# Chunked attention and an MLP on one core: pairs 3 to 5 in 64-token chunks, early transposes on another queue

## The chip, the core and the metric

The kernel runs on one core of a Trainium2 chip. The metric is the device time of one execution in microseconds. The kernel before took 215.75 us in the median of three runs (215.47 to 216.52); the profiled execution spans 214.9 us. TensorE (PE in the profile) multiplies, VectorE (DVE), ScalarE (ACT) and GpSimd (POOL) do elementwise work, SyncE (SP) issues DMAs.

## The reference

The inputs are q, k and v of 4 batches x 8 heads x 768 tokens x 64 numbers, a decay lam for each head, and the weights of an MLP with 512 inputs and 2048 hidden units. First comes a linear attention with decay, in blocks of 64 tokens with a state of 64 x 64 for each batch and head:

```
Dmask = where(rel >= 0, lam ** rel, 0)
for each block of 64 tokens:
    intra = ((qb @ kb.T) * Dmask) @ vb
    inter = (qb * lam ** (pos + 1)) @ kv_state
    out   = intra + inter
    kv_state = lam ** 64 * kv_state + (kb * lam ** (63 - pos)).T @ vb
```

The heads are then joined to rows x of 512 numbers, and each row gets a residual MLP: out = x + relu(norm(x) * g @ w1) @ w2, where norm takes off the mean and divides by the standard deviation. The reference fixes the result, not the chunk: a chunk of 128 tokens gives the same numbers as two of 64.

## The kernel before, in words

**Pairs.** The work is cut into 12 pairs (the code's u, from 0 to 11; NU is 12). A pair is 256 tokens of one batch with all heads, as two tiles of 128 rows (ab = 0 and 1). Pairs 0 to 3 are the first 256 tokens of the four batches, 4 to 7 the next, 8 to 11 the last. Pair u needs the state that pair u - 4 left.

**Two forms of the attention.** LB = 6 (L56) picks the form: pairs below it work in chunks of 128 tokens, the others in chunks of 64. In the long form, `kv` (L281) makes the state's update, `scores` (L247, two calls of 16 matmuls with 128 columns) the products of k and q, `mask` (L257) multiplies with the causal mask, `av` (L393, 64 matmuls) multiplies with v, and `inter` (L406) adds what the state gives. In the short form these are `kv64` (L346), `scores64` (L327, 32 matmuls with 64 columns), `mask64` (L333), `av64` (L380, 32 matmuls), `inter`, and `states64` (L362, L365, L287, L370), which makes a state between the chunks too. All use 64 x 64 tiles of TensorE. LB also picks how q, k and v are loaded (`fill`): below it one DMA for each tensor, with two neighbouring tokens in a partition, so rows of 512 bytes (L71); from it on two DMAs for each tensor with rows of 256 bytes (L75). `in_k`, `in_q` and `in_v` (L199, L210, L216) turn the loaded tensors to bf16, with the powers of the decay multiplied in, on GpSimd for most pairs.

**Transposes.** Attention needs k and q transposed (kqT), the MLP needs the normalised rows transposed (xT from xc). From pair 2 (xT) and pair 3 (kqT) on these are DMA transposes that SyncE issues (`to_xT`, L451; `transpose_dma`, L231), in its one queue with the loads and the stores of the output (L550), in the order of the code. [...]

**The MLP.** The two tiles of a pair make a group. `m1` has 8 units of 16 matmuls with 256 columns (L484), each followed by a relu on ScalarE (hT, L487). `m2` has 8 units of 4 matmuls with 512 columns (L522), four for each tile; after the last of a tile VectorE makes o (L543), for which `rstd_of` has to have made the standard deviation on ScalarE (std, L461) and its reciprocal on VectorE (L463). pm of both, kv64's pk and the scores of some early pairs take turns in the four PSUM buffers "mm" of `mm_tile`; a matmul that begins a new tile waits until the tile four before it in that round was read.

**The order.** There is no scheduler: the instructions of each engine run in the order in which the code records them. At the end of the kernel a list `plan` holds the units of the MLP, 16 for each group from number 22 on (group 2: 22 to 37, group 3: 38 to 53, group 4: 54 to 69), and `add(n, ...)` hangs the steps of attention, loads and transposes behind unit n. Pairs 3 to 5 have their pieces at several such places (`s1`, `s2`, `s3`, `s4`; loads by `load_one`, preparation by `p0`). Pairs from 6 on have one step, `X`, which does the end of pair u - 1 and the beginning of pair u; for pair 6 it is split into `X1` and `X2`. `wind_up` does the end of the last pair. In it a second PSUM tile, rest, takes the state's part of the odd half. `make_keep64` makes the mask of the short form on GpSimd, at unit 34.

Of the kernel before, what the change touches and what calls it, by code (L numbers as in the profile page):

```python
# [10 lines left out]
ALU = mybir.AluOpType  # L11
# [5 lines left out]
def kernel(  # L17
# [11 lines left out]
    nc = tc.nc  # L29
    B, H, S, D = q.shape  # L30
# [3 lines left out]
    NU = B * S // W  # L34
# [18 lines left out]

    half = [slice(0, 64), slice(64, 128)]
    XB = 3
    LB = 6  # L56

    def mm_tile(shape, dtype, name):
        return ps.tile(shape, dtype, tag="mm", bufs=4, name=name)
# [135 lines left out]
    def in_k(u, eng, hs=ALL):  # L195
        src = qkv_in[u]["k"][:, hs].rearrange("p (a e) j d -> p a e j d", e=2)
        dst = part(0, st[u]["kq"], hs)
        for j in range(2):
            (eng.copy if eng is nc.scalar else eng.tensor_copy)(dst[:, :, :, j], src[:, :, :, j])  # L199

    def in_q(u, eng, hs=ALL):
        src = qkv_in[u]["q"][:, hs].rearrange("p (a e) j d -> p a e j d", e=2)
        dst = part(1, st[u]["kq"], hs)
        if u < LB:
            lq = lam_q[:, hs, :].rearrange("p (a e) j -> p a e j", e=2)
        else:
            lq = lam_p[:, 0:1, hs].rearrange("p j (a e) -> p a e j", e=2).to_broadcast([128, (hs.stop - hs.start) // 2, 2, 2])
        n = (hs.stop - hs.start) // 2
        for j in range(2):
            eng.tensor_tensor(dst[:, :, :, j], src[:, :, :, j],  # L210
                              lq[:, :, :, j:j + 1].to_broadcast([128, n, 2, D]), op=ALU.mult)

    def in_v(u, eng, hs=ALL):
        n = hs.stop - hs.start
        lv = lam_v[:, hs, :, None] if u < LB else lam_p[:, 1, hs, None, None]
        eng.tensor_tensor(st[u]["vb"][:, hs], qkv_in[u]["v"][:, hs], lv.to_broadcast([128, n, 2, D]), op=ALU.mult)  # L216
# [10 lines left out]
    def transpose_dma(u):  # L227
        s = st[u]
        s["kqT"] = wk.tile([128, 2, NP, 2, 128], BF16, tag="kqT", bufs=3, name="kqT")
        for a in range(2):  # L230
            nc.sync.dma_start_transpose(s["kqT"][:, a].rearrange("p b j t -> p (b j) t"),  # L231
                                        s["kq"][:, a].rearrange("p b j e d -> p (b j e d)"))

    def scores(u, hf, early=False):
# [96 lines left out]
    def mask64(u, e):  # L331
        s = st[u]
        nc.vector.tensor_tensor(s["mA"][:, e], s["sc"][e],  # L333
                                keep64[:, None, None, :].to_broadcast([128, NP, 2, D]), op=ALU.mult)

    def kv64(u):
        s = st[u]
        last = (u // B + 1) * W >= S
        s["pk"] = [mm_tile([128, 2, NP, D], F32, f"pk{ab}") for ab in range(2)]
        n_j = (2, 1 if last else 2)  # L340
        for j in range(2):
            for p in range(NP):
                for e in range(2):
                    for ab in range(2):
                        if j < n_j[ab]:
                            nc.tensor.matmul(s["pk"][ab][half[e], j, p, :], lhsT=s["kq"][half[ab], 0, p, j, e],  # L346
                                             rhs=s["vb"][half[ab], 2 * p + e, j], start=(p == 0 and j == 0),
                                             stop=(p == NP - 1 and j == n_j[ab] - 1), skip_group_check=True)
# [93 lines left out]
    def to_xT(u, ab):  # L442
        s = st[u]
        t = 2 * u + ab
        g = group_of[t]
        i = t - groups[g][0]
        if i == 0:
            xT_of[g] = gp.tile([128, KA, GT * 128], BF16, tag="xT", bufs=3, name="xT")
        dst = xT_of[g][:, :, i * 128:(i + 1) * 128]
        if u >= 2:  # L450
            nc.sync.dma_start_transpose(dst, s["xc"][:, ab])  # L451
        else:
            xt = mm_tile([128, KA, 128], BF16, "xt")
# [243 lines left out]
    def p0(u, k_eng=None):  # L697
# [2 lines left out]
        in_q(u, nc.gpsimd)  # L700
        in_v(u, nc.gpsimd)

    def s0(u):
        kv(u, "po")
        new_state(u, 0, nc.gpsimd)
        new_state(u, 1, nc.gpsimd)
# [13 lines left out]
    def wind_up(u):  # L720


        s = st[u]
        if u < LB:
            av(u, range(NP))
        else:
            av64(u)
        inter(u, 0, fence=False)
        qT = s["kqT"][:, 1]
        has = [s["S"][ab][1] is not None for ab in range(2)]  # L730
        rest = [ps.tile([128, H, D], F32, tag="sc", bufs=2, name=f"rest{ab}") if has[ab] else None for ab in range(2)]
        for p in range(NP):
            for jq in range(2):
                for e in range(2):
                    ab = 1 - e
                    if s["S"][ab][jq] is not None:
                        nc.tensor.matmul(rest[ab][half[jq], 2 * p + e, :], lhsT=qT[half[e], p, jq, half[ab]],
                                         rhs=s["S"][ab][jq][half[e], p, :],
                                         start=(p == 0), stop=(p == NP - 1), skip_group_check=True)
        s["x"] = xp.tile([128, 2, DM], F32, tag="x", name="x")  # L740
        s["mv"] = xp.tile([128, 2, 2], F32, tag="mv", name="mv")
        s["xc"] = wk.tile([128, 2, DM], BF16, tag="xc", name="xc")
        for ab in range(2):
            x, xh = s["x"][:, ab], s["x"][:, ab].rearrange("p (a e d) -> p a e d", e=2, d=D)
            nc.scalar.copy(x, s["po"][ab].rearrange("p h d -> p (h d)"))
            if has[ab]:

                odd = xh[:, :, 1 - ab]
                nc.vector.tensor_tensor(odd, odd, rest[ab].rearrange("p (a e) d -> p a e d", e=2)[:, :, 1 - ab], op=ALU.add)
            stats = wk.tile([128, 6], F32, tag="stats", name="stats")  # L750
            nc.vector.bn_stats(stats, x)
            nc.vector.bn_aggr(s["mv"][:, ab], stats)
            nc.vector.scalar_tensor_tensor(s["xc"][:, ab], in0=x, scalar=s["mv"][:, ab, 0:1], in1=g_row,
                                           op0=ALU.subtract, op1=ALU.mult)
# [88 lines left out]
    def add(at, *steps):  # L843
        after.setdefault(at, []).extend(steps)
# [5 lines left out]
    add(6, (s2, 2))  # L850
    add(8, (s0, 2))
    add(10, (s3, 2))
    add(12, (s4, 2), (p4, 2), (p0, 3, nc.vector), (transpose_dma, 3))
    for n, name in zip((14, 15, 16), "kqv"):
        add(n, (load_one, 5, name))
    add(15, (rstd_of, 2))
    add(17, (p0, 4))
    add(25, (s1, 3))
    add(25, (transpose_dma, 4))
    add(27, (s2, 3))  # L860
    add(28, (p0, 5))
    add(29, (s3, 3))
    add(30, (s4, 3), (p4, 3))
    for n, name in zip((30, 31, 32), "kqv"):
        add(n, (load_one, 6, name))
    add(34, (rstd_of, 3), (make_keep64,))
    add(37, (transpose_dma, 5))
    add(38, (s1, 4))
    add(39, (p0, 6))
    add(40, (s2, 4))  # L870
    add(42, (s3, 4))
    add(44, (s4, 4), (p4, 4))
    add(46, (transpose_dma, 6))
    add(50, (s1, 5), (rstd_of, 4))
    add(53, (s2, 5))
    for j in range(6, NU):
        at = 55 + 16 * (j - 6)
        if j > 6:
            for n, name in zip((23, 21, 19), "kqv"):
                add(at - n, (load_one, j, name))  # L880
            add(at - 13, (p0, j))
            add(at - 8, (transpose_dma, j))
        if j < LB:
            add(at, (s1_s3, j))
            add(at + 4, (s2_s4, j), (p4, j - 1))
        else:
            if j == 6:
                add(at + 1, (X1, j))
                add(at + 5, (X2, j), (p4, j - 1))
            else:  # L890
                add(at + 2, (X, j), (p4, j - 1))
        add(at + 9, (rstd_of, j - 1))
    add(151, (wind_up, NU - 1), (p4, NU - 1))
    add(159, (rstd_of, NU - 1))
# [32 lines left out]
```

## Time and profile before

| what | value |
|---|---|
| median of three runs | 215.75 us (215.47 to 216.52) |
| TensorE busy in the profile | 201.9 us, 94% of the span |
| VectorE, ScalarE, GpSimd busy | 102.9, 87.1, 79.4 us |
| DMA queue of SyncE (q1) | 32.38 MB, 71.4% of 16 engines' span |
| chain that ended last | TensorE 75%, DMA 13%, GpSimd 4% |
| matmuls of the MLP (L484, L522) | 86.3 and 81.1 us |
| length of groups 2, 3, 4 (55.02 to 106.11 us) | 17.00, 17.91, 16.18 us |
| length of groups 5, 6, 7 | 15.36, 15.22, 15.26 us |

The length of a group is the time from its first L484 matmul to that of the next group. Groups 5 and later hold one pair of the short form each; groups 2 to 4 hold the pieces of pairs 3 to 5 and the beginning of pair 6. In the answers shown below, an arrow in brackets names what ended an engine's idle time, and the chain is followed back from the last instruction: each piece is either work or a wait for what the piece names.

### The profile page before, as it was taken

What the parts mean: (1) busy time and instruction counts of PE and PEld (TensorE: products, weight loads), DVE (VectorE), ACT (ScalarE), POOL (GpSimd) and SP (SyncE); (2) the same over time, 40 slices, a digit from 0 to 9 for tenths busy, and PEclk for the clock granted to TensorE, in tenths of its full rate; (3) what the DMA queues carried; (4) which work ended last, traced back from release to release, by engine and by line L of the source; (5) the groups of instructions that cost most, each with busy time, mean ns of one, the idle gap of its engine ahead of it and who ended that gap; (6) DMA issues with size and microseconds to landing.
All of it is one profiled execution on the core that took longest, in us unless ns stands there. A gap on an engine that the chain in (4) does not pass through costs nothing.

```text
span 214.9 us, 6642 instructions
## 1 busy us (share of the span) xinstructions
PE 201.9 (94%) x2884; PEld 138.2 (64%) x2899; DVE 102.9 (48%) x225; ACT 87.1 (41%) x165; POOL 79.4 (37%) x111
## 2 busy tenths in 40 slices
PE   2989999999799999999999999999999999999992
PEld 0568788454674675585585685784784874866861
DVE  3678461565168436747347256174183292522011
ACT  4765679120442244055063162261370460731600
POOL 4747139039464173229019138056065020000000
PEclk9999999999999999999999999999999999999998
DMA  4999999999999898799799999998998511320303
GB/s 130 289 272 207 219 263 160 236 284 234 215 303 208 169 229 153 110 215 209 126 220 199 137 230 200 177 203 198 206 246 131 128 27 27 99 52 0 98 3 95
DMA packets 94142, 37.13 MB, mean 173 GB/s; under 512 B 68385, under 2 KB 91169, under 8 KB 94114
## 3 DMA queue, kind: packets, MB, share of 16 engines
q1 hardware_dynamic: 89584, 32.38, 71.4%
q0 software_dynamic: 4224, 4.19, 12.4%
q8 instruction: 22, 0.36, 0.7%
q10 hardware_dynamic: 306, 0.14, 0.3%
q14 instruction: 6, 0.05, 0.1%
HBM read 27.27 MB, written 6.29 MB: 156 GB/s over the span
## 4 chain that ended last, share of the span: by engine, by line
PE 75%; DMA 13%; POOL 4%; SPq 3%; DVE 2%; issue 1%; POOLq 0%
PE pm L484 35%; PE pm L522 30%; DMA vin<-in_v_dram 6%; DMA qin<-in_q_dram 4%; SPq L71 3%; DMA kqT<-kq 2%; POOL kq L210 2%; POOL vb L216 2%; PE pm2h L513 2%; PE po L406 1%; PE po L393 1%; PE sc L247 1%; PE po L380 1%; PE sc L327 1%; PE pm1t L496 1%
## 5 line engine op out<-in xcount | busy, mean ns | idle before, releaser
L487 ACT ACTIVATE hT<-pm 128x512 bf16<-128x512 f32 x92 | 54.9, 601 | 91.2 <-PE pm L484 91.0
L484 PE MATMUL pm<-xT,w 128*128 128x256 bf16 x736 | 86.3, 273 | 1.9 <-DMA xT<-xc 1.2
L522 PE MATMUL pm<-w,hT 128*128 128x512 bf16 x353 | 81.1, 379 | 1.0 <-issue 0.3
L484 PEld LDWEIGHTS <-w 128*128 128x128 bf16 x736 | 69.8, 98 | 13.8 <-DMA xT<-xc 1.7
L522 PEld LDWEIGHTS <-hT 128*128 128x128 bf16 x368 | 35.5, 98 | 40.0
L543 DVE SCALAR_TENSOR_TENSOR o<-pm,rstd,x 128x512 f32<-128x512 f32 x23 | 17.1, 748 | 43.5 <-PE pm L522 43.4
L287 POOL TENSOR_TENSOR Sn<-Stmp,lam_s 128x256 bf16<-128x256 f32 x16 | 9.7, 611 | 69.7 <-DVE Stmp L365 49.0
L435 DVE SCALAR_TENSOR_TENSOR xc<-po,mv,g_row 128x512 bf16<-128x512 f32 (+1 forms) x24 | 16.8, 706 | 1.8
L257 DVE TENSOR_TENSOR mA<-sc,keep 128x512 bf16<-128x512 f32 x20 | 13.1, 685 | 6.8 <-PE sc L247 6.7
L428 ACT COPY x<-po 128x512 f32<-128x512 f32 x18 | 9.9, 588 | 11.3 <-PE po L393 5.3
L430 DVE BATCH_NORM_STATS2 stats<-x 128x6 f32<-128x512 f32 x18 | 12.4, 688 | 3.9 <-ACT x L428 3.9
L417 DVE COPY seen<-po 128x8 f32<-128x8 f32 x18 | 2.3, 162 | 23.2 <-PE po L406 23.2
L216 POOL TENSOR_TENSOR vb<-vin,lam_v 128x1024 bf16<-128x1024 f32 (+1 forms) x7 | 11.8, 1696 | 3.7 <-DMA vin<-in_v_dram 3.7
L210 POOL TENSOR_TENSOR kq<-qin,lam_q 128x512 bf16<-128x512 f32 x10 | 10.3, 1045 | 7.0 <-DMA qin<-in_q_dram 7.0
L210 POOL TENSOR_TENSOR kq<-qin,lam_p 128x512 bf16<-128x512 f32 x12 | 12.3, 1042 | 0.9 <-DMA qin<-in_q_dram 0.7
L216 POOL TENSOR_TENSOR vb<-vin,lam_p 128x1024 bf16<-128x1024 f32 x6 | 11.4, 1896 | 1.7 <-DMA vin<-in_v_dram 1.7
L199 POOL CAST kq<-kin 128x512 bf16<-128x512 f32 (+1 forms) x18 | 10.3, 599 | 0.6 <-DMA kin<-in_k_dram 0.6
L333 DVE TENSOR_TENSOR mA<-sc,keep 128x512 bf16<-128x512 f32 x12 | 8.2, 681 | 1.4 <-PE sc L327 1.4
L406 PE MATMUL po<-Sn,kqT 64*64 64x64 bf16 x216 | 7.4, 199 | 0.0
L224 PE MATMUL tp<-ident,kq 128*128 128x128 bf16 x48 | 6.2, 277 | 0.3 <-ACT kq L199 0.2
L406 PEld LDWEIGHTS <-kqT 64*64 64x64 bf16 x304 | 5.3, 108 | 1.5 <-issue 1.5
L224 PEld LDWEIGHTS <-kq 128*128 128x128 bf16 x48 | 4.1, 120 | 3.2 <-DVE kq L199 1.5
(98 smaller groups left out, 146.0 us busy)
## 6 DMA issues: line engine op xcount, KB each, us to landing
out_dram<-o SPq DMA_DIRECT2D x22, 256.0 KB, 4.5
w<-in_moe_w_ch_dram POOLq DMA_DIRECT2D x8, 512.0 KB, 9.6
kin<-in_k_dram SPq DMA_DIRECT2D x14, 256.0 KB, 3.9
qin<-in_q_dram SPq DMA_DIRECT2D x14, 256.0 KB, 5.2
vin<-in_v_dram SPq DMA_DIRECT2D x14, 256.0 KB, 5.6
kin<-in_k_dram SPq DMA_DIRECT2D x5, 512.0 KB, 6.5
qin<-in_q_dram SPq DMA_DIRECT2D x5, 512.0 KB, 8.7
vin<-in_v_dram SPq DMA_DIRECT2D x5, 512.0 KB, 7.7
```

Source lines behind the costliest of these rows:

```text
L199: (eng.copy if eng is nc.scalar else eng.tensor_copy)(dst[:, :, :, j], src[:, :, :, j])
L210: eng.tensor_tensor(dst[:, :, :, j], src[:, :, :, j], lq[:, :, :, j:j + 1].to_broadcast([128, n, 2, D]), op=ALU.mult)
L216: eng.tensor_tensor(st[u]["vb"][:, hs], qkv_in[u]["v"][:, hs], lv.to_broadcast([128, n, 2, D]), op=ALU.mult)
L224: nc.tensor.transpose(tp[:, i, j, :], s["kq"][:, a, p, j], ident)
L257: nc.vector.tensor_tensor(s[f"mA{hf}"][:, e], s[f"sc{hf}"][e], kp[:, None, :, :].to_broadcast([128, 2, 2, 128]), op=ALU.mult)
L406: nc.tensor.matmul(s["po"][ab][half[jq], 2 * p + e, :], lhsT=qT[half[e], p, jq, half[ab]], rhs=s["S"][ab][jq][half[e], p, :], start=False, ...
L430: nc.vector.bn_stats(stats, po if early else x)
L435: nc.vector.scalar_tensor_tensor(xc[:, sl], in0=po[:, sl], scalar=mv[:, 0:1], in1=g_row[:, sl], op0=ALU.subtract, op1=ALU.mult)
L484: nc.tensor.matmul(pm[:, b, :], lhsT=w1[n // W2K][:, kk, (n % W2K) * 128:(n % W2K + 1) * 128], rhs=xT_of[g][:, kk, 0:N], start=(b == 0 and ...
L487: nc.scalar.activation(hT[:, u * NB:(u + 1) * NB, 0:N], pm, ACT.Relu)
L522: nc.tensor.matmul(acc[i], lhsT=hT[:, kk, i * 128:(i + 1) * 128], rhs=w2[kk // W2K][:, kk % W2K, :], start=(kk == 0), stop=(kk == KB - 1))
L543: nc.vector.scalar_tensor_tensor(o[:, ab], in0=a, scalar=rstd[:, ab:ab + 1], in1=x[:, ab], op0=ALU.mult, op1=ALU.add)
```

## The change

Pairs 3 to 5 go to the short form as well (LB = 3). Their TensorE work comes in one or two pieces: pair 3 has a step `first64` (kv, scores, masks and states) and a `wind_up`, pair 4 a `first64` of its own and is ended by pair 5's `X`, and pairs 5 and 6 go by `X` like the later ones. With LB their loads change to rows of 256 bytes, two DMAs for each tensor. The transposes of xc of pairs 2 and 3 (XQ) and of kq of pair 3 (KQ) are issued by ScalarE and not by SyncE. Steps move to other places of the plan, GpSimd's order with them: q of pair 4 is prepared before the states of pair 3, its v after them. `make_keep64` moves ahead of pair 3's preparation. Since the first chunk of pair 3 has no state before it, rest of its first tile has one half of the rows only, which the new `rows` takes account of. The aim is less and less broken TensorE work in groups 2 to 4.

```diff
     XB = 3
-    LB = 6
+    LB = 3
+    XQ, KQ = (2, 3), (3,)
...
-            nc.sync.dma_start_transpose(s["kqT"][:, a].rearrange("p b j t -> p (b j) t"),
+            (nc.scalar if u in KQ else nc.sync).dma_start_transpose(s["kqT"][:, a].rearrange("p b j t -> p (b j) t"),
...
-            nc.sync.dma_start_transpose(dst, s["xc"][:, ab])
+            (nc.scalar if u in XQ else nc.sync).dma_start_transpose(dst, s["xc"][:, ab])
...
+    def p0_kq(u):
+        open_window(u)
+        in_k(u, nc.gpsimd)
+        in_q(u, nc.gpsimd)
+
+    def p0_v(u):
+        in_v(u, nc.gpsimd)
+
+    def first64(u):
+        kv64(u)
+        scores64(u)
+        mask64(u, 0)
+        states64(u, 0)
+        mask64(u, 1)
+        states64(u, 1)
...
-                nc.vector.tensor_tensor(odd, odd, rest[ab].rearrange("p (a e) d -> p a e d", e=2)[:, :, 1 - ab], op=ALU.add)
+                rows = slice(0, 128) if s["S"][ab][0] is not None else half[1]
+                nc.vector.tensor_tensor(odd[rows], odd[rows], rest[ab].rearrange("p (a e) d -> p a e d", e=2)[rows, :, 1 - ab], op=ALU.add)
...
-    add(12, (s4, 2), (p4, 2), (p0, 3, nc.vector), (transpose_dma, 3))
-    for n, name in zip((14, 15, 16), "kqv"):
-        add(n, (load_one, 5, name))
+    add(12, (s4, 2), (p4, 2), (make_keep64,), (p0, 3, nc.vector), (transpose_dma, 3))
     add(15, (rstd_of, 2))
-    add(17, (p0, 4))
-    add(25, (s1, 3))
-    add(25, (transpose_dma, 4))
-    add(27, (s2, 3))
-    add(28, (p0, 5))
-    add(29, (s3, 3))
-    add(30, (s4, 3), (p4, 3))
-    for n, name in zip((30, 31, 32), "kqv"):
-        add(n, (load_one, 6, name))
-    add(34, (rstd_of, 3), (make_keep64,))
-    add(37, (transpose_dma, 5))
-    add(38, (s1, 4))
-    add(39, (p0, 6))
-    add(40, (s2, 4))
-    add(42, (s3, 4))
-    add(44, (s4, 4), (p4, 4))
-    add(46, (transpose_dma, 6))
-    add(50, (s1, 5), (rstd_of, 4))
-    add(53, (s2, 5))
-    for j in range(6, NU):
+    add(16, (load_one, 5, "k"))
+    add(17, (p0_kq, 4))
+    add(20, (transpose_dma, 4))
+    add(21, (load_one, 5, "q"), (load_one, 5, "v"))
+    add(23, (first64, 3))
+    add(24, (p0_v, 4))
+    add(28, (wind_up, 3))
+    add(31, (p4, 3))
+    add(32, (first64, 4))
+    add(34, (rstd_of, 3))
+    for j in range(5, NU):
         at = 55 + 16 * (j - 6)
-        if j > 6:
+        if j > 5:
             for n, name in zip((23, 21, 19), "kqv"):
                 add(at - n, (load_one, j, name))
-            add(at - 13, (p0, j))
-            add(at - 8, (transpose_dma, j))
...
+        add(at - 13, (p0, j))
+        add(at - 8, (transpose_dma, j))
+        add(at + 2, (X, j), (p4, j - 1))
         add(at + 9, (rstd_of, j - 1))
```

More of the change, by code (lines that the diff above doesn't have):

```diff
@@ L852 @@
     add(10, (s3, 2))
-    add(12, (s4, 2), (p4, 2), (p0, 3, nc.vector), (transpose_dma, 3))
-    for n, name in zip((14, 15, 16), "kqv"):
-        add(n, (load_one, 5, name))
+    add(12, (s4, 2), (p4, 2), (make_keep64,), (p0, 3, nc.vector), (transpose_dma, 3))
     add(15, (rstd_of, 2))
-    add(17, (p0, 4))
-    add(25, (s1, 3))
-    add(25, (transpose_dma, 4))
-    add(27, (s2, 3))
-    add(28, (p0, 5))
-    add(29, (s3, 3))
-    add(30, (s4, 3), (p4, 3))
-    for n, name in zip((30, 31, 32), "kqv"):
-        add(n, (load_one, 6, name))
-    add(34, (rstd_of, 3), (make_keep64,))
-    add(37, (transpose_dma, 5))
-    add(38, (s1, 4))
-    add(39, (p0, 6))
-    add(40, (s2, 4))
-    add(42, (s3, 4))
-    add(44, (s4, 4), (p4, 4))
-    add(46, (transpose_dma, 6))
-    add(50, (s1, 5), (rstd_of, 4))
-    add(53, (s2, 5))
-    for j in range(6, NU):
+    add(16, (load_one, 5, "k"))
[9 more added lines that the diff above has]
+    for j in range(5, NU):
         at = 55 + 16 * (j - 6)
-        if j > 6:
+        if j > 5:
             for n, name in zip((23, 21, 19), "kqv"):
                 add(at - n, (load_one, j, name))
-            add(at - 13, (p0, j))
-            add(at - 8, (transpose_dma, j))
[L883 to L891, printed above, removed]
+        add(at - 13, (p0, j))
+        add(at - 8, (transpose_dma, j))
+        add(at + 2, (X, j), (p4, j - 1))
         add(at + 9, (rstd_of, j - 1))
```

## The prediction

> **What bounds the kernel now.** I read the page's busy shares first, then the chain that ended last in order of time, then the timeline of 36 to 74 us, then the DMA issues. The page says that TensorE is the bound and that the DMA engines have little room in the first three quarters:
>
> ```profile
> PE 201.9 (94%) x2884; PEld 138.2 (64%) x2899; DVE 102.9 (48%) x225; ACT 87.1 (41%) x165; POOL 79.4 (37%) x111
> ...
> PEclk9999999999999999999999999999999999999998
> DMA  4999999999999898799799999998998511320303
> ```
>
> The clock is full, so TensorE's time is work and order, not throttling. The chain is TensorE from 59 us to the end; before that it runs through a load and a transpose. This is where pairs 3 to 5 begin:
>
> ```profile
> 52.36 1.80 POOL kq L210 x2
> 54.16 5.07 DMA kqT<-kq
> 59.23 0.04 issue
> 59.27 0.42 PE sc L247 x16
> 59.69 1.85 PE pm L484 x16
> 61.55 0.35 PE sc L247 x16
> 61.89 1.85 PE pm L484 x16
> 63.75 0.64 PE po L393 x64
> ```
>
> The reader sees the 128-token form: 2 x 16 score matmuls and 64 of mA times v, in pieces between the matmuls of the MLP. Later in the same chain stands a pair in the 64-token form, all in one place:
>
> ```profile
> 106.11 3.49 PE pm L484 x32
> 109.60 0.38 PE po L380 x32
> 109.97 0.13 PE po L406 x16
> 110.10 0.32 PE pk L346 x32
> 110.42 0.29 PE sc L327 x32
> 110.72 0.16 PE po L406 x16
> 110.87 3.69 PE pm L484 x32
> ```
>
> Cut by MLP groups, the windows show what each form costs (first column: start, end, length; then PE busy):
>
> ```profile
> 55.02:72.02 17.00, 16.57 (x239) 10.79 (x241) 7.78 (x17) 6.24 (x11) 7.56 (x11) 1.00 0.98 222
> 72.02:89.93 17.91, 17.66 (x319) 11.63 (x322) 10.55 (x22) 5.94 (x11) 7.54 (x9) 1.00 0.97 178
> 89.93:106.11 16.18, 15.91 (x258) 10.75 (x259) 8.85 (x19) 6.10 (x11) 6.92 (x9) 1.00 0.89 178
> 106.11:121.47 15.36, 15.31 (x225) 10.47 (x225) 7.77 (x17) 6.05 (x11) 6.88 (x9) 1.00 1.09 188
> 121.47:136.69 15.22, 15.17 (x217) 10.50 (x217) 7.35 (x16) 6.05 (x11) 6.37 (x8) 1.00 1.03 197
> ```
>
> The MLP matmuls are the same in each; the last three columns are clock, DMA share and GB/s. The DMA share is about 1 in all of them.
>
> [...] 512 KB of a pair's tensor in 512-byte rows land about 1.77 us apart (kin of pair 3 at 45.08, vin of pair 4 at 53.93, five tensors later), while in 256-byte rows the halves land 1.2 us apart, so 2.4 us a tensor (109.85 to 115.84 us, five halves). [...] 16 matmuls of L484 take 1.75 us alone and 1.85 after a piece of 64x64 matmuls.
>
> **The change part by part.**
>
> *TensorE work of pairs 3 to 5.* The three windows sum to 17.00 + 17.91 + 16.18 = 51.09 us; three in the 64-token form would be 3 x 15.28 = 45.84. After, the first of the three windows holds more than the form: both halves of pair 3 and the first of pair 4, so one extra kv and scores (0.32 + 0.29) and two more breaks (0.1 each, as above), and the "rest" matmuls (0.1): +0.9. Saved: 51.09 - 45.84 - 0.9 = 4.35 us. The parts agree: mA times v 3 x (0.64 - 0.38) = 0.8, scores 3 x 0.4 = 1.2, seven pieces fewer of twelve at 0.1 to 0.3 each [...], 1 to 2. It is on TensorE, which sets the end: count it in full, **-4.4**.
>
> *Loads of pairs 3 to 5 in 256-byte rows.* LB also picks the row order, so nine tensors change at +0.67 us each (2.44 - 1.77). From 40 to 70 us the DMA engines are full, so nothing hides this in the queue; the question is only which landing TensorE waits for. My landings: kin 3 at 45.9, qin 3 at 48.3, vin 3 halves at 49.5 and 50.8; kin 4 halves at 52.3 and 54.1 with the transposes of the other queue in between; qin 4 near 58, vin 4 near 61 (before: 45.08, 46.67, 48.99, 50.69, 52.4, 53.93).
>
> *Transposes of pairs 2 and 3 on ScalarE's queue.* Before, SyncE reaches the transpose of xc of pair 2 only at 49.08, since it was filling the queue with pair 4's loads; it lands at 54.88 and TensorE stood 1.20 us before L484. After, ScalarE issues it, but the program's eight DMA semaphores go round in order of the code: each DMA first waits for the one eight before it. For xT of pair 2 those are the halves of vin 3 (49.5, 50.8). An issue takes 1.2 us and lands 3.5 us (median of the issues) after it began: 50.8 + 3.5 to 4.4 = 54.3 to 55.2, against 54.88. So of the 1.20 us I count **-0.3** (0 to -1.2).
>
> For kqT of pair 3 they are the halves of kin 4. ScalarE thus stands until 54.1, issues 1.3 us, is free at 55.4. Behind it on ScalarE: std (L461, 0.30), then hT of the next group. VectorE's reciprocal (L463) waits for std: 56.0; behind it on VectorE are three o (L543, 0.75 each) that free the "mm" buffers: 56.75, 57.5, 58.25. Before, std ran at 47.60 and this was long over. The built program makes the second L484 unit wait for the first of these, and kv of pair 3 for the other two. kv would start at 54.7 + 2 x 0.93 + 0.1 = 56.65 and starts at 58.25: **+1.6**. kqT lands at 54.1 + 3.3 to 5.1 = 57.4 to 59.2; scores then ask for it at 58.6, so it is mostly inside the same wait. Bounds: 0 if kin 4 lands as early as before (50.69: all is free by 53), 4 if it lands at 55 and the transpose takes the 6.46 us seen for pair 4's.
>
> *Then the pieces follow each other closely.* States of pair 3: GpSimd does q of pair 4 first (near 60), then Sn and Sm (0.61 + 0.40, twice, between VectorE's 0.43s): 63.1; the second piece needs them at 63.9: 0. kqT of pair 4 (SyncE, after out and kin 5, which wait for qin 4 and vin 4): issued 62.9 to 65.5, landing 67.5 to 69; needed at 68.0: 0 (0 to 1). xT of pair 3 on ScalarE must wait for that landing: issued 68.3 and 69.5, landing 73 to 74; needed at 72.8: **+0.5** (0 to 1.2). kqT of pair 5 waits for xT of pair 3 and for q of pair 5: landing 78.2, needed 77.8: **+0.4** (0 to 1.5). From pair 6 on SyncE's order and the plan are those of before, which keep up with 15.3 us a pair.
>
> *At nothing:* the mask's four GpSimd instructions (0.78 us in all, now near 43.4) lie in the 3.40 us in which GpSimd waits for qin 3; VectorE's copy of 0.19 lies in the wait for kin; the rows slice halves one 0.42 us add off the path.
>
> Sum: 215.75 - 4.4 - 0.3 + 1.6 + 0.5 + 0.4 = **213.5 us**.
>
> **The rivals.**
> *A. Forecast, part given back:* 213.5, holding 212.3 to 214.6.
> *B. Everything hidden.* The landings come earlier than I have them, and no wait remains: 215.75 - 4.4 - 0.3 = 211.0, with all of the xT wait 210.2. For it: DMA gaps that the trace shows, such as a share of 0.4 to 0.5 near 57 us and 70 us; against it: the share near 1 around them and the chain of semaphores.
> *C. The waits eat the gain.* 3.0 for ScalarE's stand, 0.5 + 0.6 + 0.5 for the three transposes: 211.0 + 4.6 = 215.6. For it: kqT took 6.46 us once in this stretch; every transpose now waits for one on the other queue.
> *D. The loads become the bound, slower.* Pair 5's scores wait for all nine slower tensors, 9 x 0.67 = 6.0, and 0.3 for a SyncE queue that runs dry before kin 5: 211.0 + 6.3 = 217.3. For it: the DMA rows of the page; against it: pair 5 was loaded with time to spare (kqT of pair 5 landed at 84.97, used at 86.66, and the DMA share falls to about 0.5 at 84 to 88).
>
> **How the numbers follow.** A 0.48, B 0.20, C 0.18, D 0.14. The time is A's. Under 214.7 is faster by 0.5%: A and B, 0.68; C is no change, 0.18; D slower, 0.14. The range runs from B to C with the bounds of the first wait: 210.8 to 216.3; D and a tail of B are left out.
>
> **What would show it.** The three windows near 15.3 to 17 us instead of 17.9; 88 matmuls fewer and lines of 64x64 only in them; TensorE idle before L484 or kv near 57 us, released by VectorE's o or by kqT; ScalarE's std of pair 2 near 55 instead of 47.6. If std comes near 52, B is right. If TensorE's idle time between 55 and 80 us is over 4 us, C or D is; if it names vin or qin there, D. The forecast is wrong if the transposes on ScalarE's queue pass the loads much faster, or much slower, than one shared queue suggests.

## The result and the profile after

The changed kernel takes 222.31 us in the median of four runs (220.9 to 223.14), the kernel before 215.85 on the same chip: a ratio of 1.0306, 95% interval 1.0251 to 1.0361. It is slower by about 6.5 us. Ratios and intervals, here and below, leave out every run more than 1.5% above the lowest time of its kernel, while medians and profiles take runs as they came. The forecast was 213.5, its range ended at 216.3, and even the rival on the slower side said only 217.3.

These rows of the page of the changed kernel answer to those of before (the lines named below are one higher in it: L485 is L484 of before):

```profile
PE 201.8 (91%) x2811; PEld 137.4 (62%) x2811; DVE 103.4 (47%) x226; ACT 86.8 (39%) x165; POOL 81.9 (37%) x118
...
PEclk9999999999999969999999999999999999999999
DMA  4999999999999799499999798699999512320304
```

The weight loads (PEld) are 88 fewer, as planned (2899 to 2811); the matmul records are only 73 fewer, since that of before lacks 15 of the 368 of L522. And yet TensorE is busy as long as before (201.9). The clock row says part of why: one slice has a 6, so some matmuls ran slowly. The groups of the MLP show where the time went (start, end and length of groups 2 to 6, then what each engine was busy):

```profile
55.10:78.69 23.59, 16.86 (x280) 11.02 (x281) 11.53 (x24) 6.38 (x12) 10.53 (x13) 1.00 1.00 189
78.69:95.73 17.04, 17.04 (x224) 11.27 (x225) 8.80 (x20) 6.05 (x11) 7.83 (x11) 0.90 0.94 185
95.73:111.10 15.37, 15.37 (x226) 10.47 (x225) 7.77 (x17) 6.05 (x11) 6.88 (x9) 1.00 1.17 190
111.10:127.57 16.47, 15.45 (x225) 10.48 (x224) 7.77 (x17) 5.94 (x11) 6.88 (x9) 1.00 0.98 182
127.57:142.79 15.22, 15.22 (x217) 10.51 (x216) 7.35 (x16) 6.05 (x11) 6.33 (x8) 1.00 0.92 182
```

Group 2 starts when it did before and takes 23.59 us instead of 17.00. TensorE's idle times in the timeline of this stretch (in square brackets: how long it stood, and what ended that), with kv64 of pair 4 in between:

```profile
55.10 1.03 PE L485 MATMUL pm<-xT,w 128*128 128x256 bf16 x8 [1.08 <-DMA xT<-xc]
57.02 1.03 PE L485 MATMUL pm<-xT,w 128*128 128x256 bf16 x8 [0.88 <-DVE o L544]
...
60.48 0.45 PE L328 MATMUL sc<-kqT 64*64 64x64 bf16 x32 [1.71 <-DMA kqT<-kq]
...
69.53 0.45 PE L347 MATMUL pk<-vb,kq 64*64 64x64 bf16 x32
...
78.69 5.33 PE L485 MATMUL pm<-xT,w 128*128 128x256 bf16 x32 [4.00 <-DVE Smid L363]
```

A unit of m1 is 8 matmuls, as the x8 shows (736 of L485 for 92 relus), and not 16 as it says further up. The waits of 1.08, 0.88 and 1.71 are those that the prediction spoke of. The one of 4.00 us before group 3 is new, and it has a second price: those 32 matmuls took 5.33 us, where 32 of them take 3.65 with the new place for v of pair 5 (below). The chain of waits followed back from there:

```profile
68.23 0.94 SPq L76
69.17 0.04 issue
69.21 6.37 DMA vin<-in_v_dram
...
75.71 1.90 POOL vb L217
77.61 0.58 POOL Sn L288
78.19 0.02 issue
78.21 0.43 DVE Smid L363
78.64 0.05 issue
78.69 5.33 PE pm L485 x32
```

Read it from below. The first unit of group 3 needs an "mm" buffer. Two of the four hold pk of pair 4, which kv64 had written at 69.53. In the built program the first unit of group 3 takes the first of these two and the second unit the other. They come free when VectorE has made the second Smid and Stmp of pair 4. These need the first Sn, which GpSimd makes; and GpSimd, which works in order, had v of pair 5 ahead of it and stood waiting for that load. A load that nobody needs before 84 us held up TensorE at 74.69 (78.69 - 4.00). GpSimd's own timeline shows the order:

```profile
70.69 2.16 POOL L211 TENSOR_TENSOR kq<-qin,lam_p 128x512 bf16<-128x512 f32 x2 [2.62 <-DMA qin<-in_q_dram]
75.71 1.90 POOL L217 TENSOR_TENSOR vb<-vin,lam_p 128x1024 bf16<-128x1024 f32 x1 [2.85 <-DMA vin<-in_v_dram]
77.56 0.61 POOL L288 TENSOR_TENSOR Sn<-Stmp,lam_s 128x256 bf16<-128x256 f32 x1
```

And VectorE's shows how long the second Smid waited for that Sn:

```profile
78.21 0.42 DVE L363 TENSOR_TENSOR Smid<-pk,Sn 128x256 f32<-128x256 f32 x1 [5.27 <-POOL Sn L288]
```

Two narrow windows show the clock (the column of 1.00 and 0.50):

```profile
75.40:79.20 3.80, 0.51 (x5) 0.47 (x6) 0.95 (x3) 0.00 (x0) 2.83 (x4) 1.00 0.44 86
79.20:82.60 3.40, 3.40 (x18) 2.35 (x17) 1.27 (x3) 1.19 (x2) 0.93 (x2) 0.50 1.04 215
```

After a stretch in which TensorE was nearly idle (busy for 0.51 of 3.80 us), it ran 3.41 us at half speed (79.20 to 82.61), a loss of 1.7 us. One stand does not show how long a stand has to be for that; the last section has those of the other profiles.

For the sum, the end of group 4 before has to be read as the other ends are, at the first L484 matmul in the timeline. That is 105.94; the prediction's 106.11 is from the chain, where a piece begins when the one ahead of it ends:

```profile
105.94 3.66 PE L484 MATMUL pm<-xT,w 128*128 128x256 bf16 x32
```

So groups 2 to 4 of before take 50.92 us (55.02 to 105.94) and not 51.09. The sum of the profiled spans, 214.9 to 221.1: +0.1 at the start of group 2; in groups 2 to 4 waits of 0.88 + 1.71 + 4.00 = 6.6 and 1.7 for the clock, against work saved, which is 50.92 - (56.00 - 6.6 - 1.7) = 3.2; +1.1 in group 5. Together +6.3, for the 6.2 measured.

### The profile page after: what moved, and what is told of

It is laid out like the page before. It is cut to its first block, busy times and chain, and to the rows that moved or that the text cites. A ratio compares the mean times of both kernels' runs of the same rounds, so it can differ in the third digit from the quotient of the medians.

```text
span 221.1 us, 6505 instructions
## 1 busy us (share of the span) xinstructions
PE 201.8 (91%) x2811; PEld 137.4 (62%) x2811; DVE 103.4 (47%) x226; ACT 86.8 (39%) x165; POOL 81.9 (37%) x118
## 3 DMA queue, kind: packets, MB, share of 16 engines
q0 software_dynamic: 4224, 4.19, 11.7%
q10 hardware_dynamic: 4594, 1.19, 3.7%
## 4 chain that ended last, share of the span: by engine, by line
PE 50%; DMA 20%; issue 9%; POOL 9%; SPq 8%; DVE 3%; POOLq 0%
PE pm L485 24%; PE pm L523 21%; DMA qin<-in_q_dram 6%; SPq L76 5%; DMA w<-in_moe_w_ch_dram 4%; DMA kqT<-kq 3%; DMA kin<-in_k_dram 3%; DMA vin<-in_v_dram 3%; POOL vb L217 3%; POOL kq L211 2%; SPq L72 2%; PE pm2h L514 2%; POOL Sn L288 1%; POOL kq L200 1%; PE po L381 1%
## 5 line engine op out<-in xcount | busy, mean ns | idle before, releaser
L485 PE MATMUL pm<-xT,w 128*128 128x256 bf16 x736 | 87.4, 276 | 7.0 <-DVE Smid L363 4.0
L485 PEld LDWEIGHTS <-w 128*128 128x128 bf16 x736 | 71.0, 99 | 19.8 <-DVE Smid L363 4.9
L211 POOL TENSOR_TENSOR kq<-qin,lam_p 128x512 bf16<-128x512 f32 x18 | 18.6, 1049 | 5.5 <-DMA qin<-in_q_dram 5.5
L217 POOL TENSOR_TENSOR vb<-vin,lam_p 128x1024 bf16<-128x1024 f32 x9 | 17.3, 1917 | 4.2 <-DMA vin<-in_v_dram 4.2
L436 DVE SCALAR_TENSOR_TENSOR xc<-po,mv,g_row 128x512 bf16<-128x512 f32 (+1 forms) x22 | 15.3, 702 | 1.7
L334 DVE TENSOR_TENSOR mA<-sc,keep 128x512 bf16<-128x512 f32 x18 | 12.3, 681 | 2.7 <-PE sc L328 2.7
L429 ACT COPY x<-po 128x512 f32<-128x512 f32 x16 | 8.7, 588 | 12.0 <-PE po L407 6.7
L431 DVE BATCH_NORM_STATS2 stats<-x 128x6 f32<-128x512 f32 x16 | 11.0, 685 | 0.8 <-ACT x L429 0.8
L363 DVE TENSOR_TENSOR Smid<-pk,Sn 128x256 f32<-128x256 f32 x17 | 7.2, 423 | 6.9 <-POOL Sn L288 5.3
L462 ACT ACTIVATE std<-mv,eps_t 128x2 f32<-128x2 f32 x12 | 3.6, 298 | 14.5 <-POOL kq L211 9.0
L258 DVE TENSOR_TENSOR mA<-sc,keep 128x512 bf16<-128x512 f32 x8 | 5.2, 686 | 6.3 <-PE sc L248 6.3
L371 POOL CAST Sm<-Smid 128x256 bf16<-128x256 f32 x18 | 7.2, 398 | 1.0 <-DVE Smid L363 1.0
```

The lines of the kernel that those rows point to most:

```text
L211: eng.tensor_tensor(dst[:, :, :, j], src[:, :, :, j], lq[:, :, :, j:j + 1].to_broadcast([128, n, 2, D]), op=ALU.mult)
L334: nc.vector.tensor_tensor(s["mA"][:, e], s["sc"][e], keep64[:, None, None, :].to_broadcast([128, NP, 2, D]), op=ALU.mult)
L431: nc.vector.bn_stats(stats, po if early else x)
L436: nc.vector.scalar_tensor_tensor(xc[:, sl], in0=po[:, sl], scalar=mv[:, 0:1], in1=g_row[:, sl], op0=ALU.subtract, op1=ALU.mult)
L485: nc.tensor.matmul(pm[:, b, :], lhsT=w1[n // W2K][:, kk, (n % W2K) * 128:(n % W2K + 1) * 128], rhs=xT_of[g][:, kk, 0:N], start=(b == 0 and ...
```

## The experiments

Two theories went in. G: the order of GpSimd's work is to blame (v of pair 5 ahead of the states of pair 4), with the clock behind it. L: the 256-byte loads make everything late. A third, Q, blames the second transpose queue. In the table, "rest" is the time in the profile from the moment TensorE was ready for group 2 (the group's start less the wait before it) to the end. It is given because the part before ends at 53.8 to 57.2 us in these profiles, also between kernels that are the same up to there (54.0 in the changed kernel, 57.2 in that with 14 idle matmuls), a spread as large as some effects. Each ratio is to the kernel before as measured beside it (medians of 215.9 to 216.3). Versions in which form and row size do not belong together (512-byte rows under the short form, 256-byte rows under the long one) compute other numbers than the reference and serve as measurements only. With 256-byte rows there are also two DMAs for each tensor and not one; row size and number of DMAs were not tried apart.

| kernel | median us | ratio to before, 95% | rest us |
|---|---|---|---|
| before | 215.85 | 1 | 161.1 |
| changed | 222.31 | 1.0306 (1.0251 to 1.0361) | 167.1 |
| v of pair 5 later | 220.67 | 1.0239 (1.0165 to 1.0313) | 164.0 |
| 512-byte rows | 228.75 | 1.062 (1.0543 to 1.0696) | 171.4 |
| 12 idle matmuls | 221.61 | 1.0248 (1.0166 to 1.0331) | 166.9 |
| one queue | 224.97 | 1.0386 (1.0296 to 1.0476) | 169.8 |
| 512-byte rows, one queue | 221.68 | 1.0287 (1.0236 to 1.0337) | 165.4 |
| the same, v of pair 5 later | 217.01 | 1.0014 (0.998 to 1.0047) | 161.8 |
| before, 256-byte rows | 224.71 | 1.0405 (1.0334 to 1.0477) | 166.9 |
| before, two queues | 221.17 | 1.0215 (1.0112 to 1.0318) | 163.5 |
| load order | 221.9 | 1.0256 (1.0207 to 1.0305) | 164.0 |
| load order, pair 5 later | 222.14 | 1.0283 (1.0233 to 1.0332) | 166.1 |
| 14 idle matmuls | 222.53 | 1.0309 (1.0265 to 1.0353) | 163.6 |
| before, load order | 217.8 | 1.0089 (1.0056 to 1.0122) | 161.8 |
| before, short form for pair 5 | 219.79 | 1.0125 (1.0047 to 1.0203) | 164.1 |
| before, short form for 4 and 5 | 222.17 | 1.0287 (1.0226 to 1.0349) | 167.6 |
| before, 256-byte rows for pair 5 | 219.08 | 1.0119 (1.0046 to 1.0192) | 162.6 |
| 512-byte rows, v later, 8 idle | 216.12 | 1.0012 (0.9986 to 1.0038) | 161.4 |

**v of pair 5 prepared after the states of pair 4.**

```diff
-        add(at - 13, (p0, j))
+        if j == 5:
+            add(at - 13, (p0_kq, j))
+            add(33, (p0_v, j))
+        else:
+            add(at - 13, (p0, j))
```

> The changed kernel, with v of pair 5 prepared on GpSimd after the states of pair 4 (unit 33) and not ahead of them (unit 26). Theory G (GpSimd's order: Sn of pair 4 stands behind vb of pair 5, whose vin lands at 75.58, and so the mm buffers of pair 4's pk are held): Sn of pair 4 starts near 73 instead of 77.6, TensorE's idle time before group 3 falls from 4.0 to at most 1.5 us (then xT of pair 3 is last, 76.16), the clock stays full there, L485 x32 takes 3.5 to 3.7 instead of 5.33: 222.3 - 2.5 - 1.7 = 218.1 us (217 to 219). Theory L (the slower loads of pairs 3 to 5 set the pace, whatever waits for them): the wait moves on to kv or kqT of pair 5, time no more than 1 us less.

GpSimd now makes Sn before v, and group 3 waits 0.47 and not 4.00; its 32 matmuls run at full speed:

```profile
73.67 0.61 POOL L288 TENSOR_TENSOR Sn<-Stmp,lam_s 128x256 bf16<-128x256 f32 x1
...
76.18 1.90 POOL L217 TENSOR_TENSOR vb<-vin,lam_p 128x1024 bf16<-128x1024 f32 x1
```

```profile
57.07 3.00 PE L485 MATMUL pm<-xT,w 128*128 128x256 bf16 x16 [2.85 <-DMA xT<-xc]
...
76.06 3.65 PE L485 MATMUL pm<-xT,w 128*128 128x256 bf16 x32 [0.47 <-DVE rstd L464]
```

The mechanism is shown, but the median falls by 1.6 only, less than expected, and the intervals of the two ratios overlap. In this profile xT of pair 2 was waited for 2.85 us, and the slow clock came there (16 matmuls in 3.00 us). The clock alone does not keep this kernel slow. Each timed run has its mean clock on record, and one half-speed period of 3.41 us takes 0.008 off it (1.7 of some 218 us). One of the four runs has a clock of 1.0, so no such period, and takes 220.39 us all the same, 4.3 more than before beside it (216.11).

**512-byte rows for pairs 3 to 5.**

```diff
-        if u < LB:
+        if u < 6:
```

> The changed kernel, with pairs 3 to 5 loaded in rows of 512 bytes by one DMA for each tensor as before; the attention of these pairs then works on the tokens in another order, so its numbers are not the reference's, with the same instructions on all engines. Theory L: kin 4, vin 4 and vin 5 land 2 to 6 us earlier, the waits before L485 in groups 2 and 3 go, time 213 to 215.5 us. Theory G: vin of pair 5 still is issued after kqT of pair 4 and two stores, lands no more than 2 us earlier, and Sn of pair 4 still waits for it: 219 to 221 us.

Both theories missed. The earlier loads turned an order round: in the built program xT of pair 3 on ScalarE's queue now has to wait until kqT of pair 5 on SyncE's has landed.

```profile
83.85 5.63 PE L485 MATMUL pm<-xT,w 128*128 128x256 bf16 x32 [11.01 <-DMA xT<-xc]
```

In this order the wait of one queue's transpose for the other's costs 11.0 us. It says nothing on L; the loads have to be tried on one queue.

**All transposes on SyncE.**

```diff
-    XQ, KQ = (2, 3), (3,)
+    XQ, KQ = (), ()
```

> The changed kernel with all DMA transposes on SyncE's queue (XQ and KQ empty). Theory Q (the second queue costs: ScalarE stands, transposes wait for each other across queues): the waits of 0.9 and 1.7 us in group 2 shrink, 219 to 221 us. Otherwise (the second queue makes up for the slower loads): xT of pair 2 is issued after pair 4's loads, at 53 or later, lands near 57 to 58, kqT of pair 3 near 62: 2 to 4 us more than the changed kernel, 224 to 226 us.

It did not get faster, as Q would have it. The median is 2.7 higher, with intervals that overlap, so that the second queue helps beside slow loads is likely but not shown. The profile is of the slowest of its four runs (227.65), with waits of 2.67 for xT of pair 2, 1.88 for kqT of pair 3 and 3.30 for Smid.

**512-byte rows and one queue, and with v of pair 5 later.** The first has the second and third edit, the other also the first.

> The changed kernel with 512-byte rows for the loads of pairs 3 to 5 (its tokens are then in another order than the 64-token form takes them, so its numbers are not the reference's) and all transposes on SyncE. That leaves the 64-token form and its new places alone. Theory L (the slower loads make v of pair 5 late, and with it the states of pair 4): vin of pair 5 lands before 71, no wait of over 1 us before the first matmuls of group 3, 213 to 216. Theory G (GpSimd's order is enough, whatever the loads): the wait before group 3 stays at 2 to 4 us with VectorE's Smid named, 219 to 222.

> The kernel with 512-byte rows and one queue, and also v of pair 5 prepared after the states of pair 4 (numbers not the reference's, as there). Theory L: within 0.7 us of that kernel, since v is no longer late. Theory G: 2 to 5 us below it. If what is left of waits is for kqT and xT on SyncE's queue, both kernels stay at 216 to 219 with these waits named.

GpSimd in the first of the two:

```profile
74.35 1.90 POOL L217 TENSOR_TENSOR vb<-vin,lam_p 128x1024 bf16<-128x1024 f32 x1 [1.12 <-DMA vin<-in_v_dram]
76.20 0.61 POOL L288 TENSOR_TENSOR Sn<-Stmp,lam_s 128x256 bf16<-128x256 f32 x1
```

and in the second:

```profile
73.11 0.61 POOL L288 TENSOR_TENSOR Sn<-Stmp,lam_s 128x256 bf16<-128x256 f32 x1
...
75.64 1.90 POOL L217 TENSOR_TENSOR vb<-vin,lam_p 128x1024 bf16<-128x1024 f32 x1
```

G is upheld, and L as the whole account falls: with the fast loads and GpSimd's old order the wait before group 3 is 5.19 us and the time hardly better than the changed kernel's. vin of pair 5 still lands at 74.28, since SyncE issues it only at 66.36, behind kqT of pair 4. One edit on GpSimd then brings 4.7 us in the medians (ratios of 1.0287 and 1.0014). But with all of it the short form is only as fast as before. In the second's profile, of a run of 218.36 us, xT of pair 3 is waited for, and another half-speed period follows (the clock is 0.50 from 75.70 to 79.10):

```profile
74.36 5.32 PE L485 MATMUL pm<-xT,w 128*128 128x256 bf16 x32 [2.16 <-DMA xT<-xc]
```

By the clocks on record this is so in some runs only. Nine of the 20 have 0.988 to 0.992, as one period makes it, and take 218.08 us in the mean; eleven have 0.996 or more and take 215.88. (The kernel before has 0.996 in its profile, from a slow period at the very end alone: 0.81 over the last 3.9 us.)

**The loads alone, and the queue alone, in the kernel before.**

```diff
-        if u < LB:
+        if u < 3:
```

> The kernel before with 256-byte rows, two DMAs a tensor, for the loads of pairs 3 to 5 (the tokens are in another order than the 128-token form takes them, so its numbers are not the reference's): the loads' price alone. Theory L: pieces of pairs 3 to 5 wait for kqT, 218 to 221. If the slower loads are hidden: 215.3 to 216.6.

```diff
-            nc.sync.dma_start_transpose(s["kqT"][:, a].rearrange("p b j t -> p (b j) t"),
+            (nc.scalar if u == 3 else nc.sync).dma_start_transpose(s["kqT"][:, a].rearrange("p b j t -> p (b j) t"),
...
-            nc.sync.dma_start_transpose(dst, s["xc"][:, ab])
+            (nc.scalar if u == 2 else nc.sync).dma_start_transpose(dst, s["xc"][:, ab])
```

> The kernel before with the transposes of xc of pair 2 and of kq of pair 3 issued by ScalarE: the second queue alone. If ScalarE's stand costs what the prediction reckoned, std of pair 2 comes later than 50 and 216.5 to 218; if the second queue only takes away SyncE's delay, the wait of 1.2 us before group 2 is gone and 214.3 to 215.5.

Slower loads alone cost 4.05%, and not by kqT, as L had it, but by xT. That is more than either reading expected. In the kernel before with 256-byte rows:

```profile
58.62 6.06 PE L484 MATMUL pm<-xT,w 128*128 128x256 bf16 x32 [3.95 <-DMA xT<-xc]
...
78.37 1.03 PE L484 MATMUL pm<-xT,w 128*128 128x256 bf16 x8 [0.86 <-DMA xT<-xc]
```

SyncE reached xT of pair 2 only at 53.84, after all of pair 4's loads. The second queue alone costs 2.15%, more than expected too, but in the way the prediction reckoned: std of pair 2, behind the transposes on ScalarE, comes at 59.41 (47.60 before), and o and xT are waited for:

```profile
58.38 1.55 PE L484 MATMUL pm<-xT,w 128*128 128x256 bf16 x8 [2.15 <-DMA xT<-xc]
60.60 3.53 PE L484 MATMUL pm<-xT,w 128*128 128x256 bf16 x24 [0.68 <-DVE o L543]
```

So each half hurts the old plan. The changed plan, which has both, is no slower than the loads alone make the old one (1.0306 against 1.0405, with intervals that just overlap).

**Another order of the loads.** In a version of each plan q and v of pair 4 are issued behind xT of pair 2; in that of the changed one all transposes are on SyncE and v of pair 5 is later, as above. A further version also has q of pair 5 later on GpSimd and its load earlier. The edit as the changed plan has it:

```diff
-    load_window(4)
+    load_one(4, "k")
...
-    add(12, (s4, 2), (p4, 2), (make_keep64,), (p0, 3, nc.vector), (transpose_dma, 3))
+    add(12, (s4, 2), (p4, 2), (load_one, 4, "q"), (load_one, 4, "v"), (make_keep64,), (p0, 3, nc.vector), (transpose_dma, 3))
```

> The changed kernel with all transposes on SyncE, the loads of q and v of pair 4 moved behind the transpose of xc of pair 2, and v of pair 5 prepared after the states of pair 4. Theory T (the loss is waits that come from the order of SyncE and GpSimd, and the TensorE clock that falls after them): the wait for xT before group 2 (1.1 to 2.9 in the kernels so far) is gone or under 0.5, std of pair 2 comes before 50, no wait over 1 us before group 3, 213 to 216. Rival (the 256-byte loads set the pace whatever the order): a wait of 2 us or more stays in groups 2 or 3, 218 to 221.

> As the kernel with the new order of loads, and q and v of pair 5 prepared after the states of pair 4, q of pair 5 loaded ahead of the transpose of kq of pair 4, and pair 5's step one unit later. Theory T: at or under that kernel, 211.5 to 214.5. Rival: kqT of pair 5 comes too late by what its preparation was moved (about 1 us) and it stays at 215 or over.

> The kernel before with the loads of q and v of pair 4 moved behind the transpose of xc of pair 2: the order of the loads without the 64-token form. If the wait of 1.2 us before group 2 goes and nothing else comes late: 214.3 to 215.2 where the kernel before has 215.8. If pair 4 now comes late: 216 to 218.

The wait for xT of pair 2 is gone in all three, as expected, and comes back elsewhere. In the first:

```profile
62.77 0.45 PE L328 MATMUL sc<-kqT 64*64 64x64 bf16 x32 [4.19 <-DMA kqT<-kq]
...
80.01 3.65 PE L485 MATMUL pm<-xT,w 128*128 128x256 bf16 x32 [1.36 <-DMA xT<-xc]
```

Its transpose of kq of pair 3 was being issued from 55.56 to 59.52, while v of pair 4 was still landing. In the further version the wait is 5.25, in the old plan 1.32. Here the rival is upheld: in these three orders another transpose is late instead. The windows of groups 2 to 4 of the first also give the form's worth, once the waits are taken off:

```profile
56.30:80.01 23.71, 17.95 (x279) 11.84 (x280) 11.92 (x24) 6.05 (x11) 10.93 (x16) 0.93 1.09 191
80.01:95.37 15.36, 15.31 (x223) 10.45 (x225) 7.02 (x16) 6.05 (x11) 8.25 (x10) 1.00 0.95 192
95.37:110.73 15.36, 15.31 (x224) 10.45 (x224) 7.76 (x17) 6.05 (x11) 6.92 (x9) 1.00 0.98 190
```

Less 4.19, 1.36 and 1.7 for the clock these are 47.2 us, 3.7 under 50.92.

**The short form for fewer pairs, and the loads of one pair.** In the kernel before, LB = 5 and LB = 4, with pair 5 in one piece (pair 4 in two) and pair 6 by X; then 256-byte rows for pair 5 alone. The edit for LB = 5:

```diff
-    LB = 6
+    LB = 5
...
-    add(50, (s1, 5), (rstd_of, 4))
-    add(53, (s2, 5))
+    add(50, (rstd_of, 4))
+    add(52, *[(kv64, 5), (scores64, 5), (mask64, 5, 0), (states64, 5, 0), (mask64, 5, 1), (states64, 5, 1)])
...
-            if j == 6:
+            if j == 0:
```

> The kernel before with the 64-token form for pair 5 too (LB = 5), in one piece at unit 52, and pair 6 by one step X. If the loads of the early pairs are the cause and pair 5 has time to spare (its kqT landed 1.7 us before its use): a third of the work saved, 1.2 to 1.5 us, less what its three slower loads cost: 214.4 to 215.8. If the form itself or its slower loads cost here too: 217 to 219.

> The kernel before with the 64-token form for pairs 4 and 5 (LB = 4), each in one or two pieces near their old places, all transposes on SyncE. If the loads are the cause, pair 4 already pays: its kqT comes about 2 us later and scores of pair 4 wait 1 to 2.5 us, against 2.5 us of work saved: 215 to 217. If the form gains wherever it is used: 213 to 214.

> The kernel before with 256-byte rows for the loads of pair 5 alone (tokens in another order than its form takes them, so its numbers are not the reference's). If pair 5 has room: within 0.7 us of before, 215.8 to 216.7. If the three tensors cost a third of what nine cost (8.5): 218 to 219.

All three are slower: their intervals lie above 1, though the ratio of two of them is under 1.02. Even three slow tensors cost 1.2%, with runs from 215.92 to 222.25. The spare time that the prediction saw (kqT of pair 5 landed 1.7 us early) is not where it hurts: the loads of pair 5 stand ahead of xT of pair 3 in the queue. In the profiles, which are of runs above the median (219.73, 220.09 and 224.83), xT is waited for 2.35 us before group 3 with slow loads for pair 5 alone, 2.77 with LB = 5 and 3.37 with LB = 4, and half speed follows (8 matmuls of L484 in 1.87 us, 16 in 3.22 and 16 in 3.59, where 8 take 1.03 and 16 take 1.9 at full speed). By the clocks on record two of six, one of six and none of six runs are without it.

**Idle matmuls against the slow clock.** The changed kernel with 12 and with 14 matmuls whose result nothing uses, behind group 2; and 8 of them in the kernel with 512-byte rows, one queue and v of pair 5 later.

```diff
+    add(37, (keep_busy, 14, "po0"))
```

> The changed kernel, with 12 matmuls of 512 columns of constants into an unused PSUM tile behind the last MLP unit of group 2, where TensorE stood 4.0 us. If the idle time is what lowered the clock: the 12 take 2.6 us of the idle time, the clock keeps 1.0, L485 x32 takes 3.5 to 3.7 us instead of 5.33, time 1.5 to 1.8 us less, 220.6 us. If the slow matmuls have another cause: same time as the changed kernel within 0.3 us.

> The changed kernel with 14 idle matmuls of 128x512 behind group 2, where TensorE stood for 4.0 us; 12 of them took 2.75, so these fill about 3.2. Their result is used by nothing. If the clock of TensorE falls because it stood still: no half-speed period near 79 us, the next 32 matmuls take 3.5 to 3.9 instead of 5.33, 220.2 to 221. If the half speed has another cause: 222 to 223.

> The kernel with 512-byte rows, one queue and v of pair 5 after the states of pair 4 (numbers not the reference's), with 8 idle matmuls of 128x512 behind group 2, where TensorE stood 2.16 us for xT of pair 3 and then ran one period of 3.41 us at half speed. The idle matmuls take about 1.8. If standing still brings the half speed: no half-speed period near 76 to 79 us and 1 to 1.7 us less than that kernel's 217.0. If not: the same time within 0.5 us, or more.

With 12 the wait behind them was still 4.75 us in that profile and the 32 matmuls took 5.33, so that profile decides nothing. With 14:

```profile
76.12 3.18 PE L587 MATMUL idle<-keep_h,ident 128*128 128x512 bf16 x14
80.61 3.67 PE L485 MATMUL pm<-xT,w 128*128 128x256 bf16 x32 [1.30 <-DVE Smid L363]
```

With 8, where without them the 32 had taken 5.32:

```profile
72.20 1.89 PE L587 MATMUL idle<-keep_h,ident 128*128 128x512 bf16 x8
75.14 3.65 PE L485 MATMUL pm<-xT,w 128*128 128x256 bf16 x32 [1.05 <-DMA xT<-xc]
```

In both no half-speed period comes there (3.67 and 3.65 us for the 32), so it was the stand that brought it. The clocks of the timed runs agree: 11 of 20 runs have 0.996 or more without the 8, and 20 of 22 with them. The time followed less clearly. With 8 the median is 0.9 lower, since the runs of 218 become rare. But runs without a half-speed period are no faster with the 8 than without (216.15 and 215.88 in the mean), and the ratios (1.0012 and 1.0014) don't tell the two apart. With 14 the median is not lower at all, though the rest in its profile is 3.5 us shorter: before group 2, where this edit changes nothing, that profile had lost 3.1 us, part of it in a half-speed period at 24.5 to 27.9 us (16 matmuls of L485 from 24.75 took 3.43). The clocks of its six runs (0.985 to 0.992) leave room for a period in each; where it lay in those without a profile is open.

The profile with the 8 also shows where the kernel without slow loads and slow clock still loses what the form saves. Groups 2 to 4:

```profile
56.06:75.14 19.08, 17.82 (x286) 11.66 (x289) 10.84 (x23) 6.05 (x11) 8.78 (x14) 1.00 1.11 208
75.14:90.51 15.37, 15.31 (x224) 10.47 (x225) 7.36 (x17) 6.05 (x11) 8.73 (x10) 1.00 1.07 200
90.51:105.87 15.36, 15.31 (x224) 10.47 (x224) 7.77 (x17) 6.05 (x11) 6.88 (x9) 1.00 1.03 185
```

Less the idle matmuls (1.89) and the wait behind them (1.05) these are 46.9 us, 4.0 under before's 50.92. Of that, 2.9 are lost again before group 3, until xT of pair 3 lands; 0.8 ahead of group 2, where xT of pair 2 is waited for 1.97 and not 1.20; and 0.6 in group 5.

## Why the prediction was wrong

**The step that failed** is "Then the pieces follow each other closely", in the item on states. It looked at GpSimd's order for pair 3 ("States of pair 3: GpSimd does q of pair 4 first ... 0", which was right: av64 at 65.33 did not wait) and did not ask it of pair 4. There v of pair 5 stands ahead of Sn, its load lands at 75.6, and until Sn is made, pk holds two of four "mm" buffers. Measured: 4.0 us, where the sum has no term. The next step, that a wait of 4 us costs more than itself, was missing too: 1.7 us of half speed. Together these are 5.7 of the 8.8 us between forecast and result. The rest is mis-sized terms, and 1.1 in group 5.

- *TensorE's work, -4.4.* Right in kind, and near in size: -3.2 in this profile, -3.7 in the one with the new load order, -4.0 in the one with 8 idle matmuls. 0.2 of the difference is the misread end of group 4. Groups 3 and 4 come to 15.3 to 15.4 each without waits and clock, as reckoned (15.28). Group 2 is 17.0 here, 16.5 and 16.1 in the other two, and was reckoned at 16.2; where its 0.8 in the changed kernel come from is open.
- *xT of pair 2, -0.3.* It landed at 54.97, inside the forecast's 54.3 to 55.2; the wait fell from 1.20 to 1.08. The landing came true by luck: its second half was issued at 48.88, 2 us earlier than forecast, and took 6.1 us from there, where 3.5 to 4.4 were reckoned.
- *ScalarE's stand, +1.6.* Right in what waits: std came at 55.82 (forecast near 55), and o was waited for. Why ScalarE stood so long was wrong, and the time came out by luck: kin of pair 4 landed by 51.13 and not 54.1, but issuing the second transpose took 3.07 us (52.70 to 55.77) and not 1.3. So the bound "all is free by 53" if kin 4 is early does not hold. The size was 0.88 + 1.71 = 2.6, because kqT landed at 60.44 and not by 59.2 (7.7 us after its issue began, for 3.3 to 5.1 reckoned), so the two waits did not overlap.
- *kqT of pair 4, 0.* Right: no wait at 69.80.
- *xT of pair 3, +0.5.* It landed at 76.16, 1.5 after TensorE was ready; this lies inside the 4.0.
- *kqT of pair 5, +0.4.* 0: it landed at 80.85, asked for at 84.65, since all was late by then.
- *Loads.* The landings of pairs 3 and 4 were 1.6 to 3.3 us earlier than forecast (vin 4 at 58.10, not 61), so the loads were reckoned too slow and the transposes beside them too fast.
- *"From pair 6 on keeps up".* Group 5 has 1.1 more than before (16.47), with a wait of 1.02 before L485 put down to VectorE. The other profiles with the short form from pair 3 on have 15.4 to 16.65 there, and VectorE's work up to there lies at the same places relative to the group's start as before. Its cause is open.

The rivals: D had the right side, for loads as the bound and vin at the head of the chain, but reckoned it through pair 5's scores and at 6.3 us. The loads by themselves cost 8.5 in the old plan, through xT. No rival went through GpSimd's order. The prediction's own sign, over 4 us of idle time between 55 and 80, did point to C or D (it was 6.6, without group 2's first wait).

What is shown: the wait of 4.0 us is GpSimd's order, and the half-speed period comes from the wait. With that order the kernel stays slower than before even with the old loads and one queue (221.68 us), and there one edit of it brings 4.7 us. The loads cost 8.5 us in the old plan, and with them the kernel stays slower even with the better order (220.67, 1.6 less, within the noise). So each suffices to undo the gain, and they hide each other. With both undone the kernel is at the time of before, not under it, since transposes are still late. No version tried was faster than before.

## What to carry to other kernels

When steps are moved, go through every in-order engine and ask of each instruction what it waits for and what stands behind it; do it for each round of the loop, not for the first alone. An early preparation of data for later is harmless to what stands behind it only if its load is sure to have landed: v of pair 5, which landed at 75.58, held Sn until 77.56 and TensorE for 4.00 us. Ask also what the loads stand ahead of in their queue: loads that have spare time themselves, such as pair 5's here, may still delay a transpose that is on the path (xT of pair 3, waited for 2.35 us with slow loads for pair 5 alone).

## What the runs showed of the hardware

- In the changed kernel's profile the clock behind the stand of 4.00 us was 0.50 for 3.41 us (79.20 to 82.61), and 1.00 on both sides of it. In the other profiles half speed shows in the time of the matmuls behind a stand: of L485 (L484 in the old plan), 8 took 1.03 us at full speed, 16 took 1.91, 32 took 3.65 and 40 took 4.53.
- From group 2 on no stand of TensorE of up to 1.97 us was followed by slow matmuls, if it came alone (16 in 1.91 behind the one of 1.97, 32 in 3.67 behind one of 1.72). Those of 2.15, 2.16, 2.35, 2.77, 2.85 and more were (8 in 1.55, 32 in 5.32, 8 in 1.87, 16 in 3.22, 16 in 3.00), but for one of 2.67 (16 in 1.91), after which the slow matmuls came only with a second stand of 1.88 shortly behind (40 in 6.21).
- The price was 1.7 us behind the stands of 2.16, 4.00 and 4.75 (32 in 5.32 to 5.33), and 2.0 to 2.9 behind those of 11.01, 5.19, 3.95 and 3.30 (5.63, 5.66, 6.06 and 6.58).
- Issuing a DMA transpose took 1.19 us of the engine's queue at the least and 3.07 at the most in the profiles of before and after. In the kernel before with two queues the two issues of kqT of pair 3 on ScalarE took 6.05 (53.31 to 59.36), the second of them 4.6 (from 54.73), while loads of pairs 3 and 4 were landing (55.70 to 60.21).
- With 256-byte rows and two DMAs a tensor the five tensors behind kin of pair 3, up to vin of pair 4, landed within 14.0 us (44.08 to 58.10, changed kernel), with 512-byte rows and one DMA within 8.9 (45.08 to 53.93, before), the first with transposes among them.
